# One pass of a fused linear-attention and mixture-of-experts kernel: the state added by an identity matmul, fewer matmuls of zeros, and steps put in other places

## The chip, the cores and the metric

The kernel runs on one core of a Trainium2 chip. Its time is device microseconds of one execution; 482.89 us is the median of three runs. A profiled execution is a run of its own, with a time of its own.

## The reference, cut to what matters

A gated linear attention is followed by a mixture of eight experts that takes one expert for each token. Batch is 4, heads 8, sequence 768, head width 48, model width 384, hidden width 1024.

```python
for t in range(S):                       # attention: a state of 48 x 48 per head
    state = alpha[:, :, t, :, None] * state + einsum('bhd,bhe->bhde', k[:, :, t], v[:, :, t])
    y[:, :, t] = einsum('bhd,bhde->bhe', q[:, :, t], state)
...
logits = einsum('bsd,de->bse', x, w_gate)            # x is y with the heads side by side
...
    e = argmax(logits[b, s]) if s == 0 or local_gate[b, s] < 0.5 else prev_e
    p = softmax(logits[b, s])
    out[b, s] = p[e] * (maximum(x[b, s] @ w1[e], 0) @ w2[e])
```

## The kernel before, in words

**The attention blocks.** The 3072 tokens are cut into 24 blocks of 128 (`NB`), four at a time from the four batches (`G`), so that block i continues the state of block i-4. A block is two chunks of 64 tokens. The loop over i (line 684) works on several blocks at once. In pass i it does, in this order: `one_a(i+2)` (GpSimd writes ones into the decay tile `a`), `scan2(i+1)` (VectorE's backward scan `sf`, after which GpSimd multiplies k), `flush` (work put off on the list `later`), `kt(i)` (k transposed by TensorE into `kp`, copied by ScalarE to `kk`), `copies(i-1)` and `state(i-1)`, `pm(i)` (scores `pe`, masked to `pq` by VectorE), some of the list `made`, a first `other()`, `scan1(i+2)` (VectorE's forward scan `A`, after which GpSimd multiplies q), loads, `xt(i-2)` (y transposed into `xp`, copied to `xx`), `ym(i-1)` (the output `y`: first scores times values, `y<-vt,pq`, then q times state, `y<-sb,x`), `first_v(i+1)`, a step of the weights, a second `other()`, `um(i)` (k times v into the PSUM tile `up`), a third `other()`.

**The state.** `um` (line 369) makes 8 matmuls into `up`, which holds two sums for each head: over the first chunk and over the whole block. VectorE then adds the old state to both (line 387) into the SBUF tile `st`. `copies` (line 390) lets ScalarE copy the two results into `sb` in two instructions, and `state` (line 395) multiplies the last one with the decay for block i+4. `up` is one PSUM buffer.

**The order.** From line 658 on every engine's instructions are pinned to program order, so each engine is a queue in which a waiting instruction holds all behind it.

**other(), line 622.** It runs `flush`, then one step of each generator in `steps` (the routing of a group of four blocks, `route`, line 432, which yields between its steps), and then, while `work[0]` is empty, `DN` matmuls of zeros (`dense`, line 293: 128x128 weights, 256 columns, into the PSUM tile `h2`). When the routing of the third group ends, `work[0]` becomes `early()` (line 562): early expert work on the first 1536 tokens. It comes in pieces: gathers, empty pieces, two transposes (`trans`, into `tp`, in the same PSUM buffer as `kp` and `xp`), eight pieces of the first layer (`gemm1`: 9 matmuls into a half of `h2`, a relu by ScalarE to `hh`, and a remainder `hl` that VectorE computes at the next `flush`), then pieces of the second layer (`yp`). In passes 0 to 23 a second and a third `other()` take one piece each, from pass 24 on all three do.

**After the blocks.** `while steps` (line 728) goes on until the last group is routed. The other experts follow (lines 753 to 768), with 480 tokens each.

**At the start** (lines 264 to 282 and 647 to 683) GpSimd clears tiles and builds constants before it writes the first `one_a(0)`; a list `made` of 12 further ones is spread over the first passes, three in each.

Of the kernel before, what the change touches and what calls it, by code (L numbers as in the profile page):

```python
# [46 lines left out]
DN = 2  # L47
# [19 lines left out]
def gla_moe(ctx, tc, akq, vw, vn, wg, w1, w2, cst, tok, out):  # L67
# [188 lines left out]
    with ExitStack() as ac, ExitStack() as aa:  # L256
# [16 lines left out]
        for j in range(2):  # L273
            sb = ap.tile([R, 2, 2, CW], F32, bufs=1, name=f"sb{j}")
            g_.memset(sb[0:64], 0.0)
            g_.memset(sb[64:112, :, 1, :], 0.0)
            SBs.append(sb)
            oh = ap.tile([128, E, G + 1], F32, bufs=1, name=f"oh{j}")
            g_.memset(oh, 0.0)
            OHs.append(oh)  # L280

        st = {"c": c0}
        sts = [ap.tile([R, 3, HP, D], F32, tag="st", bufs=G + 1, name=f"st_{i}") for i in range(G)]
# [35 lines left out]
        def scan1(i):  # L319
# [7 lines left out]
            q2 = x[:, BW:].rearrange("p (s t) -> p s t", t=C)  # L327
            g_.tensor_tensor(q2, q2, A.rearrange("p (s t) -> p s t", t=C + 1)[:, :, 1:], ALU.mult)
            d["k"] = x[:, 0:BW].rearrange("p (h t) -> p h t", h=HP)
            d["q"] = x[:, BW:2 * BW].rearrange("p (h t) -> p h t", h=HP)  # L330

# [37 lines left out]
        def um(i):  # L369
# [3 lines left out]
            if i < G:  # L373
                s3 = sts[i]
                g_.memset(s3[:, 0], 0.0)
            else:
                s3 = st["S", i % G]
            uw = pp.tile([128, 512], F32, tag="up", name=f"up_{i}")
            up = uw[0:R, 0:2 * CW].rearrange("p (h c d) -> p c h d", c=2, h=HP)
            for hp in range(HP):  # L380
                n = slice(2 * hp * D, 2 * (hp + 1) * D)
                t_.matmul(uw[64:112, n], lhsT=kk[:, hp, 64:112], rhs=vt[:, :, 2 * hp * D:(2 * hp + 1) * D],
                          start=True, stop=True)
                t_.matmul(uw[0:64, n], lhsT=kk[:, hp, 0:64], rhs=vt[:, :, (2 * hp + 1) * D:(2 * hp + 2) * D],
                          start=True, stop=True)
            n = 2 if i + G < NB else 1
            v_.tensor_tensor(s3[:, 1:1 + n], up[:, 0:n], s3[:, 0].unsqueeze(1).broadcast_to([R, n, HP, D]), ALU.add)
            d["s3"] = s3

        def copies(i):  # L390
            sf, sb = blk[i]["s3"].rearrange("p c h d -> p c (h d)"), blk[i]["sb"]
            s_.copy(sb[64:112, :, 0, :], sf[64:112, 0:2])
            s_.copy(sb[0:48, :, 1, :], sf[0:48, 0:2])

        def state(i):
            d = blk[i]
            if i + G < NB:
                sn = ap.tile([R, 3, HP, D], F32, tag="st", bufs=G + 1, name=f"st_{i + G}")
                v_.scalar_tensor_tensor(sn[:, 0], d["s3"][:, 2], 1.0 / SEED,
                                        d["end"].unsqueeze(2).broadcast_to([R, HP, D]), ALU.mult, ALU.mult)  # L400
                st["S", i % G] = sn
# [30 lines left out]
        def route(g):  # L432
# [36 lines left out]
            yield  # L469
# [29 lines left out]
            yield  # L499
            v_.tensor_tensor(ex, ex, ob, ALU.mult)  # L500
            pn = rt([128, n], "pn")
            v_.tensor_reduce(pn, ex, AX.X, ALU.add)
            v_.tensor_tensor(pl[:, :, 0], pn, se, ALU.mult)
# [5 lines left out]
            yield  # L509
            ps = rt([128, E, n + 1], "ps")  # L510
# [28 lines left out]
            else:  # L539
                for j in range(n):  # L540
                    s_.activation(on[:, j], iob, AF.Abs, bias=rr[:, j:j + 1], scale=-1.0)
                    s_.activation(on[:, j], on[:, j], AF.Relu, bias=one[:, 0:1], scale=-float(TS))
                    if j < n - 1:
                        yield
# [17 lines left out]
        def early():  # L562
# [10 lines left out]
            for _ in range(4):  # L573
                yield False
# [47 lines left out]
        def other(pieces=True):  # L622
# [5 lines left out]
            if work[0] is None:  # L628
                if DN:
                    dense(DN)  # L630
            else:
                if last and drained[0]:
                    last[0].ht, last[0].yt = HL, YL
                for done in work[0] if pieces else ():
                    if done or steps or not drained[0]:
                        break

# [9 lines left out]
        g_.memset(one, 1.0)  # L647
        g_.memset(m5, 1.0)
        g_.memset(m5[:, :, 0], 0.0)
        for e in range(E):  # L650
            g_.memset(c0[:, e:e + 1], float(e * RS - 1))
            g_.memset(c1[:, e:e + 1], float(e * RS - 1 + (C1 if e in EARLY else 0)))
        g_.tensor_copy(trif, cc("tri"))
        g_.memset(trif[0:64, 64:128], 1.0)
        g_.memset(trif[64:128, 0:64], 0.0)
# [4 lines left out]
        made = [  # L660
            lambda: g_.memset(fill, 0.0),
# [279 lines left out]
```

## Time and profile before

| what | value |
|---|---|
| runs | 481.34, 482.89 and 493.2 us, median 482.89 |
| profiled execution, its own time | 484.0 us |
| its span, first to last instruction | 482.2 us, 10873 instructions |
| mean granted TensorE clock | 0.961 |
| ScalarE, GpSimd busy | 194.1 us, 186.7 us |
| HBM read and written | 55.84 MB, 10.62 MB |

A row of a group of instructions says: line, engine, operation, result <- sources, shape, count, then the busy time in us and the mean of one in ns, then the idle time of the engine just before them and what ended it. PE is TensorE, DVE VectorE, ACT ScalarE, POOL GpSimd, SP the queue of loads. All compute instructions carry line 81, the helper that records them, so they are told apart by their tiles. A row of a timeline begins with its start and its duration in us. A row of stretches gives, for each stretch of the span, its length and then the busy time and the count for PE, PE's weight loads, DVE, ACT and POOL, and at the end the granted clock, the share of DMA and GB/s. Busy times of PE are modelled, and pipelined matmuls overlap: the distance from one start to the next says what one costs.

### The profile page before, as it was taken

How to read it: one execution, taken by the hardware profiler on the slowest of the kernel's cores; microseconds unless marked ns; L12 is line 12 of the kernel's file. 1: busy time of each engine (PE TensorE's matmuls, PEld its weight loads, DVE VectorE, ACT ScalarE, POOL GpSimd, SP SyncE). 2: the span in 40 equal slices, each digit the busy share in tenths (PEclk: the TensorE clock that was granted, in tenths of full speed). 3: DMA queues.
4: the chain of work that ended last, by engine and by line, in shares of the span. 5: the costliest groups of instructions: out<-in, count | busy, mean ns of one | idle time of the engine just before them, and what ended most of it. 6: DMA issues, size and time to landing. Idle time of an engine off the chain costs nothing.

```text
span 482.2 us, 10873 instructions
## 1 busy us (share of the span) xinstructions
PE 437.9 (91%) x4443; PEld 391.5 (81%) x4443; DVE 257.3 (53%) x485; ACT 194.1 (40%) x390; POOL 186.7 (39%) x207
## 2 busy tenths in 40 slices
PE   5999898999997978698989999999999999999990
PEld 5777776878875877597878998998989989989990
DVE  4778999898997235722274445244254252342310
ACT  1345656565756436321354324335144233242210
POOL 6654326364556000261053642724732503504201
PEclk9799999999998899888899999999999999999997
DMA  8789767596661102660075554444351542531100
GB/s 217 199 260 252 222 187 201 164 292 167 189 208 50 51 17 71 180 186 27 1 224 188 134 181 138 124 131 123 114 175 57 158 130 65 174 98 39 50 3 27
DMA packets 26710, 66.01 MB, mean 137 GB/s; under 512 B 4384, under 2 KB 10677, under 8 KB 26658
## 3 DMA queue, kind: packets, MB, share of 16 engines
q1 hardware_dynamic: 18672, 49.65, 36.3%
q0 software_dynamic: 3840, 10.62, 6.9%
q10 hardware_dynamic: 4146, 5.03, 3.1%
q8 instruction: 35, 0.57, 0.5%
q14 instruction: 17, 0.14, 0.1%
HBM read 55.84 MB, written 10.62 MB: 138 GB/s over the span
## 4 chain that ended last, share of the span: by engine, by line
PE 53%; issue 11%; DVE 9%; ACT 3%; POOL 2%; POOLq 0%; DVEq 0%; ACTq 0%
PE h L81 24%; PE yp L81 20%; PE y L81 3%; PE tp L81 2%; DVE A L81 2%; POOL out L81 1%; PE up L81 1%; DVE st L81 1%; DVE sf L81 1%; DVE pq L81 1%; ACT hh L81 1%; POOL w1l_0b L81 1%; PE pe L81 1%; DVE xl L81 1%; PE lp L81 1%
## 5 line engine op out<-in xcount | busy, mean ns | idle before, releaser
L81 DVE SCALAR_TENSOR_TENSOR hl<-h,hh 128x480 fp32r<-128x480 f32 (+2 forms) x80 | 43.9, 556 | 77.2 <-ACT hh L81 76.9
L81 ACT ACTIVATE hh<-h 128x480 fp32r<-128x480 f32 (+2 forms) x80 | 38.7, 490 | 82.4 <-PE h L81 82.3
L81 POOL DMA_INDIRECT out<-yo,idx x32 | 32.5, 1017 | 80.5 <-DVE yo L81 78.0
L81 POOL DMA_INDIRECT xg<-xd,idx x32 | 32.6, 1018 | 61.0 <-PE tp L81 52.9
L81 DVE TENSOR_SCALAR yo<-yp,acc 128x384 f32<-128x384 f32 (+1 forms) x32 | 19.6, 616 | 61.1 <-PE yp L81 61.0
L81 POOL TENSOR_TENSOR x<-x,sf 112x512 f32<-112x512 f32 x24 | 29.0, 1209 | 42.5 <-DVE sf L81 42.5
L81 POOL TENSOR_TENSOR x<-x,A 112x512 f32<-112x512 f32 x24 | 31.8, 1327 | 29.0 <-DVE A L81 6.6
L81 DVE TENSOR_TENSOR_SCAN A<-a,z 112x520 f32<-112x520 f32 x24 | 34.5, 1437 | 5.6 <-POOL a L81 5.6
L81 PE MATMUL h<-dz 128*128 128x256 f32 x142 | 35.0, 354 | 2.1 <-DVE z L81 2.1
L81 DVE TENSOR_TENSOR_SCAN sf<-a,z 112x520 f32<-112x520 f32 x24 | 33.8, 1408 | 0.1
L81 ACT COPY sb<-st 48x384 f32<-48x384 f32 x48 | 24.5, 510 | 11.5 <-DVE st L81 10.9
L81 PEld LDWEIGHTS h<-dz 128*128 128x128 f32 x142 | 23.8, 224 | 6.5 <-DVE z L81 2.1
L81 PEld LDWEIGHTS y<-vt,pq 64*64 64x64 f32 x768 | 24.9, 138 | 4.0 <-issue 3.8
L81 PE MATMUL y<-vt,pq 64*64 64x48 f32 x768 | 27.9, 224 | 0.0
L81 PE MATMUL y<-sb,x 112*64 112x96 f32 x384 | 21.8, 258 | 4.3 <-ACT sb L81 4.2
L81 PE MATMUL up<-vt,kk 128*48 128x96 f32 (+1 forms) x384 | 23.1, 267 | 0.0
L81 PEld LDWEIGHTS y<-sb,x 112*64 112x64 f32 x384 | 17.2, 140 | 6.2 <-ACT sb L81 5.2
L81 PEld LDWEIGHTS up<-vt,kk 128*48 128x48 f32 (+1 forms) x384 | 18.3, 140 | 3.4 <-issue 1.0
L81 ACT COPY kk<-kp 128x448 f32<-128x448 f32 x24 | 12.8, 531 | 20.7 <-PE kp L81 20.6
L81 PE MATMUL h<-xh,w1h_1a 128*128 128x256 f32 (+1 forms) x48 | 16.4, 342 | 3.9 <-DVE hl L81 2.7
L81 ACT COPY XR<-y 128x384 f32<-128x384 f32 x24 | 11.5, 479 | 20.1 <-PE y L81 20.1
L81 ACT CAST xh<-tp 128x384 fp32r<-128x384 f32 (+1 forms) x32 | 14.0, 462 | 13.9 <-PE tp L81 13.6
(247 smaller groups left out, 1234.8 us busy)
## 6 DMA issues: line engine op xcount, KB each, us to landing
x<-akq SPq DMA_DIRECT2D x24, 448.0 KB, 5.6
a<-akq SPq DMA_DIRECT2D x24, 227.9 KB, 4.5
vt<-vn SPq DMA_DIRECT2D x24, 192.0 KB, 2.7
xd<-XR ACTq DMA_DIRECT2D x24, 192.0 KB, 4.8
rw_0a<-w SPq DMA_DIRECT2D x3, 512.0 KB, 4.9
rw_0a<-w SPq DMA_DIRECT2D x4, 384.0 KB, 4.2
rw_1a<-w SPq DMA_DIRECT2D x3, 512.0 KB, 5.9
rw_1a<-w SPq DMA_DIRECT2D x4, 384.0 KB, 3.5
```

Of the source, the lines that this page charges most:

```text
L81: r = f(*a, **k)
```

## The change

The parts of the diff, in its order:

- Filler: `DN` goes from 2 to 1, and `other` takes the number as an argument, 2 for the first of a pass. So a pass issues 2 + 1 + 1 = 4 matmuls of zeros in place of 6. The test is new too: they are issued wherever no full piece of early work ran and the blocks aren't over (`not done and not drained[0]`), also after the early work has begun.
- Start: the clearing of the second `sb`, of both `oh`, `one`, `m5` and `trif` goes into `made`, which is now worked off five at a time; `c0` and `c1` are computed from `ioa` in place of sixteen small memsets; for block 0 the multiplication of q comes after that of k (`scale_q`).
- State: from block 4 on a matmul with the 112x112 identity as weights and the old state as moving operand (each head's 48 columns given twice, 384 in all, fp32) writes the state into both sums of `up`, and the 8 matmuls of `um` accumulate onto it. VectorE's addition is gone. `copies` makes four instructions of 48x192: the first chunk's state comes straight from the SBUF state, the second's from `up`. `state` reads `up`.
- Routing: two empty or nearly empty steps are dropped, the product of probabilities with the one-hot goes to GpSimd (`eo`), its sum moves behind the prefix matmul, and `on` is made two columns in a step. A group takes 12 calls in place of 16. `early` has two empty pieces in place of four.
- Weights: the step of the first early expert's weights moves behind the second `other()`, with its ScalarE cast and, at the next `flush`, its VectorE subtraction.

```diff
--- before.py
+++ after.py
@@ -44,7 +44,7 @@
 NEXT = 2
 
 DN0 = 32
-DN = 2
+DN = 1
 HL = ("h", "h", "up", "pe")
 YL = ("yp", "y")
 RT = "rt"
@@ -272,15 +272,14 @@
             VTs.append(vt)
         for j in range(2):
             sb = ap.tile([R, 2, 2, CW], F32, bufs=1, name=f"sb{j}")
-            g_.memset(sb[0:64], 0.0)
-            g_.memset(sb[64:112, :, 1, :], 0.0)
+            if j == 0:
+                g_.memset(sb[0:64], 0.0)
+                g_.memset(sb[64:112, :, 1, :], 0.0)
             SBs.append(sb)
-            oh = ap.tile([128, E, G + 1], F32, bufs=1, name=f"oh{j}")
-            g_.memset(oh, 0.0)
-            OHs.append(oh)
+            OHs.append(ap.tile([128, E, G + 1], F32, bufs=1, name=f"oh{j}"))
 
         st = {"c": c0}
-        sts = [ap.tile([R, 3, HP, D], F32, tag="st", bufs=G + 1, name=f"st_{i}") for i in range(G)]
+        sts = [ap.tile([R, HP, D], F32, tag="st", bufs=G + 1, name=f"st_{i}") for i in range(G)]
         blk = {}
         grp = {}
         later = []
@@ -324,10 +323,15 @@
             v_.tensor_tensor_scan(A, a[:, 0:SW], z1, 0.0, ALU.mult, ALU.add)
             d["end"] = A[:, 2 * C + 1:SW:2 * (C + 1)]
             v_.reciprocal(z2[0:R, 2 * C + 1:SW:2 * (C + 1)], d["end"])
-            q2 = x[:, BW:].rearrange("p (s t) -> p s t", t=C)
-            g_.tensor_tensor(q2, q2, A.rearrange("p (s t) -> p s t", t=C + 1)[:, :, 1:], ALU.mult)
+            d["A"] = A
+            if i:
+                scale_q(i)
             d["k"] = x[:, 0:BW].rearrange("p (h t) -> p h t", h=HP)
             d["q"] = x[:, BW:2 * BW].rearrange("p (h t) -> p h t", h=HP)
+
+        def scale_q(i):
+            q2 = blk[i]["x"][:, BW:].rearrange("p (s t) -> p s t", t=C)
+            g_.tensor_tensor(q2, q2, blk[i].pop("A").rearrange("p (s t) -> p s t", t=C + 1)[:, :, 1:], ALU.mult)
 
         def one_a(i):
             a = blk[i]["a"]
@@ -370,33 +374,35 @@
 
             d = blk[i]
             kk, vt, sb = d["kk"], d["vt"], d["sb"]
-            if i < G:
-                s3 = sts[i]
-                g_.memset(s3[:, 0], 0.0)
-            else:
-                s3 = st["S", i % G]
             uw = pp.tile([128, 512], F32, tag="up", name=f"up_{i}")
             up = uw[0:R, 0:2 * CW].rearrange("p (h c d) -> p c h d", c=2, h=HP)
+            if i < G:
+                st["S", i] = sts[i]
+                g_.memset(sts[i], 0.0)
+            else:
+                t_.matmul(uw[0:R, 0:2 * CW], lhsT=ident[0:R, 0:R],
+                          rhs=st["S", i % G].unsqueeze(2).broadcast_to([R, HP, 2, D]), start=True, stop=False,
+                          skip_group_check=True)
             for hp in range(HP):
                 n = slice(2 * hp * D, 2 * (hp + 1) * D)
                 t_.matmul(uw[64:112, n], lhsT=kk[:, hp, 64:112], rhs=vt[:, :, 2 * hp * D:(2 * hp + 1) * D],
-                          start=True, stop=True)
+                          start=i < G, stop=True, skip_group_check=True)
                 t_.matmul(uw[0:64, n], lhsT=kk[:, hp, 0:64], rhs=vt[:, :, (2 * hp + 1) * D:(2 * hp + 2) * D],
-                          start=True, stop=True)
-            n = 2 if i + G < NB else 1
-            v_.tensor_tensor(s3[:, 1:1 + n], up[:, 0:n], s3[:, 0].unsqueeze(1).broadcast_to([R, n, HP, D]), ALU.add)
-            d["s3"] = s3
+                          start=i < G, stop=True, skip_group_check=True)
+            d["up"], d["S"] = up, st["S", i % G]
 
         def copies(i):
-            sf, sb = blk[i]["s3"].rearrange("p c h d -> p c (h d)"), blk[i]["sb"]
-            s_.copy(sb[64:112, :, 0, :], sf[64:112, 0:2])
-            s_.copy(sb[0:48, :, 1, :], sf[0:48, 0:2])
+            d = blk[i]
+            sb = d["sb"].rearrange("p c e (h d) -> p c e h d", h=HP)
+            for c, x in ((0, d["S"]), (1, d["up"][:, 0])):
+                s_.copy(sb[64:112, c, 0], x[64:112])
+                s_.copy(sb[0:48, c, 1], x[0:48])
 
         def state(i):
             d = blk[i]
             if i + G < NB:
-                sn = ap.tile([R, 3, HP, D], F32, tag="st", bufs=G + 1, name=f"st_{i + G}")
-                v_.scalar_tensor_tensor(sn[:, 0], d["s3"][:, 2], 1.0 / SEED,
+                sn = ap.tile([R, HP, D], F32, tag="st", bufs=G + 1, name=f"st_{i + G}")
+                v_.scalar_tensor_tensor(sn, d["up"][:, 1], 1.0 / SEED,
                                         d["end"].unsqueeze(2).broadcast_to([R, HP, D]), ALU.mult, ALU.mult)
                 st["S", i % G] = sn
 
@@ -466,7 +472,6 @@
             v_.scalar_tensor_tensor(m2, kr[:, 1, :, 0], 16.0, m2, ALU.mult, ALU.add)
             v_.tensor_tensor(kr[:, 0], ge, m2.unsqueeze(2).broadcast_to([128, n, 8]), ALU.is_equal)
             yield
-            yield
 
             rp = pp.tile([8 * n, 2, 128], F32, tag=RT, name=f"rp_{g}")
             for j in range(2):
@@ -496,17 +501,17 @@
             v_.tensor_reduce(se, ex, AX.X, ALU.add)
             v_.tensor_scalar_add(se, se, 1e-9)
             v_.reciprocal(se, se)
-            yield
-            v_.tensor_tensor(ex, ex, ob, ALU.mult)
-            pn = rt([128, n], "pn")
-            v_.tensor_reduce(pn, ex, AX.X, ALU.add)
-            v_.tensor_tensor(pl[:, :, 0], pn, se, ALU.mult)
+            eo = rt([128, n, 8], "eo")
+            g_.tensor_tensor(eo, ex, ob, ALU.mult)
             yield
             pw = pp.tile([128, E, n + 1], F32, tag=RT, name=f"pw_{g}")
             t_.matmul(pw.rearrange("p e b -> p (e b)"), lhsT=one, rhs=oi.rearrange("p e b -> p (e b)"),
                       start=True, stop=False)
             t_.matmul(pw[:, :, 0:n], lhsT=trif, rhs=o4, start=False, stop=True)
             yield
+            pn = rt([128, n], "pn")
+            v_.tensor_reduce(pn, eo, AX.X, ALU.add)
+            v_.tensor_tensor(pl[:, :, 0], pn, se, ALU.mult)
             ps = rt([128, E, n + 1], "ps")
             v_.tensor_tensor(ps, pw, st["c"].unsqueeze(2).broadcast_to([128, E, n + 1]), ALU.add)
             po = rt([128, n, 8], "po")
@@ -540,7 +545,7 @@
                 for j in range(n):
                     s_.activation(on[:, j], iob, AF.Abs, bias=rr[:, j:j + 1], scale=-1.0)
                     s_.activation(on[:, j], on[:, j], AF.Relu, bias=one[:, 0:1], scale=-float(TS))
-                    if j < n - 1:
+                    if j == 1:
                         yield
             yield
 
@@ -570,8 +575,8 @@
                 j.load_list(0)
             for _ in jobs[0].gather():
                 yield False
-            for _ in range(4):
-                yield False
+            yield False
+            yield False
             for _ in jobs[0].trans():
                 yield True
             for n, j in enumerate(jobs):
@@ -619,21 +624,21 @@
 
         last, EW, steps = [], {}, []
 
-        def other(pieces=True):
+        def other(pieces=True, dn=DN):
 
             flush()
             for r in list(steps):
                 if next(r, 0) == 0:
                     steps.remove(r)
-            if work[0] is None:
-                if DN:
-                    dense(DN)
-            else:
+            done = False
+            if work[0] is not None:
                 if last and drained[0]:
                     last[0].ht, last[0].yt = HL, YL
                 for done in work[0] if pieces else ():
                     if done or steps or not drained[0]:
                         break
+            if not done and not drained[0]:
+                dense(dn)
 
         work, drained = [None], [False]
         for i in range(3):
@@ -644,20 +649,21 @@
                 nc.scalar.dma_start(cs, cst)
                 nc.scalar.dma_start(tk, tok)
                 nc.scalar.dma_start(wgs, wg[:, :, 0:32])
-        g_.memset(one, 1.0)
-        g_.memset(m5, 1.0)
-        g_.memset(m5[:, :, 0], 0.0)
-        for e in range(E):
-            g_.memset(c0[:, e:e + 1], float(e * RS - 1))
-            g_.memset(c1[:, e:e + 1], float(e * RS - 1 + (C1 if e in EARLY else 0)))
-        g_.tensor_copy(trif, cc("tri"))
-        g_.memset(trif[0:64, 64:128], 1.0)
-        g_.memset(trif[64:128, 0:64], 0.0)
         nc.scalar.dma_start(xd[0:1], z2[127:128, 0:DM])
         first_v(0)
         pinned[0] = True
         dense(DN0)
         made = [
+            lambda: g_.memset(SBs[1][0:64], 0.0),
+            lambda: g_.memset(SBs[1][64:112, :, 1, :], 0.0),
+            lambda: g_.memset(one, 1.0),
+            lambda: g_.memset(OHs[0], 0.0),
+            lambda: g_.memset(OHs[1], 0.0),
+            lambda: g_.memset(m5, 1.0),
+            lambda: g_.memset(m5[:, :, 0], 0.0),
+            lambda: g_.tensor_copy(trif, cc("tri")),
+            lambda: g_.memset(trif[0:64, 64:128], 1.0),
+            lambda: g_.memset(trif[64:128, 0:64], 0.0),
             lambda: g_.memset(fill, 0.0),
             lambda: g_.tensor_copy(fill.bitcast(I32)[:, 1:2], tk[0:SL, 2 * NB:]),
             lambda: g_.memset(acc, 0.0),
@@ -674,10 +680,16 @@
                                      tk[:, 0:2 * NB].rearrange("p (b j t) -> p t j b", b=G, t=2)[:, 0],
                                      -float(SENT), None, ALU.add),
             lambda: g_.tensor_copy(vals[:, :, 2], tk[:, 1:2 * NB:2]),
+            lambda: v_.tensor_scalar(c0, ioa[:, :, 0], WH, float(TS), ALU.subtract, ALU.mult),
+            lambda: v_.tensor_scalar(c0, c0, -1.0, None, ALU.add),
+            lambda: g_.tensor_copy(c1, c0),
+        ] + [
+            lambda e=e: g_.memset(c1[:, e:e + 1], float(e * RS - 1 + C1)) for e in EARLY
         ]
         one_a(0)
         scan1(0)
         scan2(0)
+        scale_q(0)
         one_a(1)
         scan1(1)
         wsteps = iter(())
@@ -696,9 +708,9 @@
                 pm(i)
             if i > NB:
                 drained[0] = True
-            for _ in range(min(3, len(made))):
+            for _ in range(min(5, len(made))):
                 made.pop(0)()
-            other(i >= NB)
+            other(i >= NB, 2)
             if i + 2 < NB:
                 scan1(i + 2)
             if i + 3 < NB:
@@ -717,11 +729,11 @@
             if i == W0:
                 begin(EARLY[0], v_)
                 wsteps = EW[EARLY[0]].steps()
-            elif i > W0 + 2:
-                next(wsteps, None)
             if i == T1:
                 begin(EARLY[1], v_)
             other()
+            if i > W0 + 2:
+                next(wsteps, None)
             if i < NB:
                 um(i)
             other()
```

## The prediction

> **What bounds the kernel now.** I read the page, then the span cut where blocks begin (16.5 us is where block 1's k is transposed, 40.6 block 5, 89 block 12, 126.5 block 18, 137.1 block 20, 171.1 pass 24, 201.3 the second early expert's first matmul).
>
> ```profile
> span 482.2 us, 10873 instructions
> PE 437.9 (91%) x4443; PEld 391.5 (81%) x4443; DVE 257.3 (53%) x485; ACT 194.1 (40%) x390; POOL 186.7 (39%) x207
> ...
> 0.00:16.50 16.50, 11.65 (x91) 10.61 (x92) 9.83 (x12) 2.74 (x4) 10.49 (x44) 0.83 0.93 228
> 16.50:40.60 24.10, 21.74 (x434) 18.16 (x434) 18.06 (x28) 11.29 (x23) 13.18 (x24) 0.98 0.81 236
> 40.60:89.00 48.40, 43.48 (x834) 36.34 (x833) 43.46 (x82) 29.78 (x66) 21.51 (x24) 0.96 0.68 197
> 89.00:126.50 37.50, 36.37 (x725) 30.60 (x723) 34.24 (x77) 23.46 (x58) 18.52 (x19) 1.00 0.76 222
> 126.50:137.10 10.60, 10.48 (x222) 8.87 (x220) 10.36 (x20) 6.99 (x18) 6.54 (x9) 1.00 0.66 191
> 137.10:171.10 34.00, 28.99 (x485) 23.99 (x485) 20.33 (x50) 16.82 (x42) 11.80 (x10) 0.90 0.27 82
> 171.10:201.30 30.20, 22.90 (x206) 20.37 (x206) 17.56 (x51) 15.04 (x33) 2.92 (x3) 1.00 0.29 85
> ```
>
> The share of 53% for DVE hides that it is busy 34.24 of 37.5 us from block 12 to 17, and 10.36 of 10.6 in blocks 18 and 19. But PE is fuller still: 36.37 of 37.5. So between 40.6 and 137.1 PE idles only 6.2 us of 96.5 (4.9, 1.1 and 0.1). PE's idle time lies at the start (4.9), before block 5 (2.4), and above all after 137.1 (5.0 and 7.3). What is taken from DVE pays only where PE waits, and what is given to PE is paid in full where it doesn't. What comes after 208.8 (the last stretch quoted below) is not edited, and I let it move along unchanged.
>
> **Price of the state's matmul against the fillers.**
>
> ```profile
> 118.79 0.88 PE L81 MATMUL up<-vt,kk 128*48 128x96 f32 x16
> 119.60 0.51 PE L81 MATMUL h<-dz 128*128 128x256 f32 x2
> 119.94 0.55 PE L81 MATMUL kp<-cs,x 112*128 112x112 f32 x4
> ```
>
> The groups that the edit touches:
>
> ```profile
> L81 PE MATMUL h<-dz 128*128 128x256 f32 x142 | 35.0, 354 | 2.1 <-DVE z L81 2.1
> L81 ACT ACTIVATE on<-on,one 128x128 f32<-128x128 f32 x20 | 8.0, 402 | 0.6
> L81 DVE TENSOR_TENSOR ex<-ex,oh 128x32 f32<-128x32 f32 x3 | 1.8, 602 | 0.0
> L81 DVE TENSOR_TENSOR st<-up,st 112x384 f32<-112x384 f32 x20 | 10.9, 547 | 7.2 <-POOL a L81 3.8 <-PE up L81 1.8 <-POOL st L81 1.5
> L81 ACT COPY sb<-st 48x384 f32<-48x384 f32 x48 | 24.5, 510 | 11.5 <-DVE st L81 10.9
> ```
>
> No fp32 matmul of 384 columns is there. The nearest row is `up`: 8 calls give 16 instructions, so fp32 is two passes, and they take 119.60 - 118.79 = 0.81 us. If the two column halves (64 and 48 wide) stream side by side, that is 4 x 96 = 384 columns twice, just what the identity needs, with 16 weight loads against 2: I take 0.75. If they do not, the 0.81 us stand for 16 x 96 = 1536 columns and the identity's 768 cost half of it, 0.41. Bounds 0.41 to 0.81. A pair of fillers costs 119.94 - 119.60 = 0.34, so 0.17 to 0.215 each with what follows; I take 0.19. The 142 are 32 at the start and 2 x 55. After, I count 4 in each of passes 0 to 18, 3 in pass 19 and 2 in passes 20 to 23: 32 + 76 + 3 + 8 = 119. So the label is true for a pass, but passes 18 to 23 get fillers that they didn't have, and each block from 4 on gets 0.75 - 2 x 0.19 = +0.37 us of PE work, from pass 20 on 1.13.
>
> DVE loses 24 additions (0.55 us for 20 of them). ACT's two copies of 0.51 become four of half the length; by the fixed part of an instruction I put them 0.2 us longer in all (0 to 0.5), hidden behind PE's y matmuls, except in the pass where `on` now comes as 2 + 2 columns: eight instructions of 0.4 us in one pass, where three of the four columns used to fall in one pass, with the last in the next.
>
> **Steps that only move.** The weights' step issues a load on SP's queue, a cast on ACT and, one flush later, a subtraction on DVE. On SP nothing of `other` stands between, so loads keep their order. On ACT the cast now goes behind the routing's copies or `on`, and the next `kk` waits behind it as before. On DVE the subtraction used to stand before the addition and the next sf; it still stands before sf. GpSimd's `eo` (128x32; VectorE's `ex<-ex,oh` took 0.60 us for it) runs behind q's product and is read two steps later, so it costs nothing while GpSimd is as free as it is (18.5 us of 37.5); without that cover the prefix step would come 0.6 us or more later in each of six groups. The `made` list puts 15 more small instructions into passes 0 to 5, on GpSimd mostly (the memset of `a` below took 0.11 us), behind k's products. I cost all these at nothing.
>
> **The start (-2.3; -1.5 to -3).**
>
> ```profile
> 2.15 6.41 PE L81 MATMUL h<-dz 128*128 128x256 f32 x32 [2.15 <-DVE z L81]
> 11.25 1.01 PE L81 MATMUL kp<-cs,x 112*128 112x112 f32 x4 [2.70 <-POOL a L81]
> ```
>
> ```profile
> 6.20 0.11 POOL L81 MEMSET a<- 112x4 f32 x1
> 10.02 1.17 POOL L81 TENSOR_TENSOR x<-x,sf 112x512 f32<-112x512 f32 x1 [1.18 <-DVE sf L81]
> ```
>
> VectorE's queue, and the time that loads of `a` take:
>
> ```profile
> 6.34 1.24 DVE L81 TENSOR_TENSOR_SCAN A<-a,z 112x520 f32<-112x520 f32 x1 [4.23 <-POOL a L81]
> 7.83 2.11 DVE L81 TENSOR_TENSOR_SCAN sf<-a,z 112x520 f32<-112x520 f32 x1
> ...
> DMA to landing us min/median/max: 3.1/4.5/8.2
> ```
>
> The first scan waits for the memset of `a`, which waits behind GpSimd's constants. With these gone, the load ends it: at about 4.1 if it takes near the shortest time, as nothing else is in flight. Then A runs at 4.2, sf at 5.65, in 1.24 and not 2.11 as q's product no longer runs beside it, k's product 6.9 to 8.1, block 0's transposes at 8.2 in place of 11.25. q's product and the memset for block 1 follow, so block 1 gains less: its A at 9.45, sf to 13.0, product to 14.2 in place of 16.5.
>
> **Blocks 1 to 4 (-2.4; -1 to -3).** DVE's addition waited here for GpSimd's memset of the state (3.8 + 1.5 us in the `st` row above). Nothing on DVE waits for it any more; ScalarE's copies are next in line, a pass later. PE's work falls by eight fillers (-1.5) and rises by one identity (+0.75), so its 2.4 us of idle time may go.
>
> **Blocks 5 to 17 (+3.2; 0 to +6).** 13 identities at 0.75 less 26 fillers at 0.19 are +4.8, and the list matmul of the third group now falls in here (+0.9). Against it stand the waits:
>
> ```profile
> PE lt L81 <- ACT lc L81: 1.7, 3, 0.8
> PE y L81 <- ACT sb L81: 1.5, 2, 1.1
> ```
>
> and the stretches in which PE's clock was granted at half:
>
> ```profile
> 10.85:17.68 6.83, 6.43 (x74) 5.31 (x78) 6.07 (x6) 1.16 (x3) 4.28 (x9) 0.50 1.03 268
> 58.64:62.05 3.41, 3.41 (x24) 2.84 (x24) 2.71 (x4) 1.54 (x3) 1.23 (x2) 0.50 0.98 305
> 154.20:161.00 6.80, 6.80 (x75) 6.15 (x71) 1.43 (x9) 2.84 (x7) 1.79 (x2) 0.50 0.20 61
> 202.00:208.80 6.80, 6.08 (x29) 5.61 (x28) 2.38 (x8) 1.15 (x3) 4.73 (x5) 0.50 0.83 241
> ```
>
> Of the 6.0 us that PE idles here (4.9 + 1.1) I take 4 as gone: `lt` waited for a small copy behind the weights' cast, which now stands after it, the waits for `sb` went back to the addition, and one cold stretch (1.7 us) may not come again. New is +1.5 from ACT where `on` comes in fours: three passes at 0.5.
>
> **Blocks 18 and 19 (+2.0; +1 to +3).** Two identities, five fillers and a transpose piece more, less the list matmul that has moved up: 1.5 + 0.95 + 0.45 - 0.9.
>
> **Blocks 20 to 23 (+5.0; +2 to +7).**
>
> ```profile
> 149.96 0.49 PE L81 MATMUL tp<-cs,xg 128*128 128x128 f32 x3
> 152.31 0.57 PE L81 MATMUL kp<-cs,x 112*128 112x112 f32 x4 [1.86 <-issue]
> ...
> 176.21 1.17 PE h L81 x9
> ```
>
> Early work starts four places sooner and has two empty pieces less, so by the end of pass 23 seven first-layer pieces are done in place of three. PE gets 4 x 1.2 for them, 3.0 of identities and 1.5 of fillers, less a transpose piece (0.45): +8.85. The half-rate stretch from 154.2 to 161 halves 6.8 us, worth 3.4; with this much work about, I take it as gone. Waits stay about as they are (-0.45): `kp` shares its buffer with `tp`, so the 1.86 us wait moves to pass 20 with the piece, and the fillers write `h2`, which now holds early results, so they wait for `hl`.
>
> **Pass 24 to the second expert (-8.7; -5 to -11), and the stretch after 202 (-1.7; 0 to -3.4).**
>
> ```profile
> PE lp L81 <- DVE on L81: 2.5, 1, 2.5
> PE h L81 <- DVE hl L81: 1.9, 2, 0.9
> PE rb L81 <- DVE em L81: 1.6, 1, 1.6
> ```
>
> The four pieces are gone from here (-4.8), with them the wait for `hl` (-1.9), and the last group's routing has two steps fewer while the weights' subtractions, which hold DVE before `em` and `on`, come earlier (-2.0 of 4.1). Half of the cold stretch at 202, which follows the 2.5 us wait, is counted as saved.
>
> The sum is -2.3 - 2.4 + 3.2 + 2.0 + 5.0 - 8.7 - 1.7 = -4.9. The profiled execution took 484.0, 1.1 above the median, so I subtract from the median: 478.0.
>
> **A rule beside the rows.** The 2 us of the stretch at 58.64 were lost although PE's waits for `sb` up to block 17 were 1.1 us at the longest. The Trainium skill, page "TensorE: Matmul & The Clock Gate", section "Why this matters for your kernels", tells to leave no idle gaps of more than about 3 us between bursts of matmuls; fewer fillers would then be harmless here, since no wait quoted here is that long, and the sum would not change. The trace disagrees: shorter waits were enough, so I keep a stretch more or less in the bounds.
>
> **The rivals.**
>
> 1. Slower: `up` is held longer. Before, `um` could start when the addition had read `up`; now it needs the last ScalarE copy and DVE's `state`, which stands behind a weights' subtraction, a routing step and the next sf. Price: 1 us in each of the seven blocks with a weights' step and half in each of the other eight or so, 11 in all: 489. It decides once DVE's queue from one `um` to `state` is longer than PE's block of 6 us. For it speaks DVE's 43.46 of 48.4 us; against it that DVE loses 0.55 us a block.
> 2. Faster: idle time collapses. The first, second and fourth cold stretch vanish wholly (a further -2, -1.7, -1.7), and 4 us more of the waits after 137.1: 478 - 9.4, about 469. For it: DVE's release, early work as filler. Against it: PE is full without it.
> 3. The tail is bound by the last group's chain and by the weights' casts, not by PE: pieces done early only lengthen waits, so -8.7 becomes -3: 484. For it: PE idles 7.3 of 30.2 us there. Against: that chain starts only after PE's work in pass 24.
> 4. The identity is cheap (0.41): 20 x 0.34 less, 471.
>
> **How the numbers follow.** Forecast 478: 0.40 (own range 473 to 483). Rival 1: 0.20, 2: 0.18, 3: 0.12, 4: 0.10. About 2% (473.2 and 492.5) is what a measurement of this kernel can tell from no change. Faster: 0.15 of 2, 0.08 of 4 and 0.06 of the forecast's lower end, 0.29. Slower: 0.12 of rival 1, when it adds to the upper bounds of blocks 5 to 23. Within: 0.59. The range 466 to 489 holds the forecast, 2, 3 and 4 nearly whole and the lower half of 1.
>
> **What would show it.** Right: block 0's transposes near 8.2, fillers 119, an identity matmul at 0.75 in distance of starts, PE idle below 5 us in blocks 5 to 17 and that stage longer than 85.9 us, blocks 18 and 19 near 12.6, the second expert's first matmul near 196 to 198. Wrong: `um` waiting for `state` or `sb` (rival 1); no stretch at half rate after the start (rival 2); a wait for `on` or `em` above 4 us (rival 3).

## The result and the profile after

The changed kernel takes 508.1 us, the median of four executions from 506.1 to 510.2, against 486.4 for four of the kernel before. The ratio is 1.054, 95% interval 1.045 to 1.063: slower by 5%. The profiled execution took 510.21 us, its span 508.4, 26.2 more than the span before. Some executions, here and in the experiments, ran at a lower granted clock and took longer, and every ratio leaves them out (here 489.95 and 493.2 of the kernel before, in r1 four of seven); the profiled executions of r1, r3 and b3 were of that kind, so lengths are not taken from them.

The stretches of the span of the changed kernel, cut where the same blocks begin (columns as before: length, busy time and count of PE, its weight loads, DVE, ACT and POOL, granted clock, DMA share, GB/s):

```profile
0.00:15.50 15.50, 8.81 (x89) 7.88 (x89) 8.70 (x12) 2.84 (x4) 7.59 (x17) 1.00 0.89 240
15.50:41.70 26.20, 25.62 (x429) 20.89 (x429) 19.02 (x27) 12.01 (x30) 15.62 (x37) 0.80 0.71 202
41.70:95.80 54.10, 48.63 (x835) 38.17 (x834) 41.03 (x76) 33.43 (x82) 20.10 (x28) 0.91 0.65 185
95.80:147.00 51.20, 45.17 (x731) 35.92 (x731) 32.77 (x66) 25.97 (x71) 21.84 (x24) 0.87 0.55 164
147.00:161.80 14.80, 12.56 (x228) 9.76 (x227) 10.76 (x23) 7.58 (x21) 4.74 (x8) 1.00 0.64 190
161.80:198.00 36.20, 35.62 (x534) 29.38 (x534) 15.16 (x40) 18.65 (x51) 8.63 (x10) 0.91 0.16 51
198.00:225.20 27.20, 19.72 (x177) 17.39 (x176) 16.63 (x47) 14.49 (x32) 3.64 (x4) 0.99 0.45 124
225.20:508.40 283.20, 261.61 (x1450) 241.72 (x1449) 101.48 (x167) 87.51 (x148) 101.89 (x76) 0.96 0.35 108
```

Against the rows of before the stages differ by -1.0, +2.1, +5.7, +13.7, +4.2, +2.2, -3.0 and +2.3. The loss stands in the third to fifth: blocks 5 to 19 take 23.6 us more. There PE's idle time (length less busy) grew from 4.9, 1.1 and 0.1 us to 5.5, 6.0 and 2.2, and the clock fell from 0.96 and 1.00 to 0.91 and 0.87. PE, full before, now waits and runs slowly.

Of TensorE's waits in the changed kernel the four longest, and of VectorE's the one that is new (total, times, longest), one fence each:

```profile
PE lp L81 <- POOL a L81: 7.3, 3, 2.5
PE rp L81 <- DVE kr L81: 5.8, 5, 1.7
PE kp L81 <- POOL x L81: 4.0, 2, 2.6
PE lp L81 <- DVE on L81: 3.8, 1, 3.8
```

```profile
DVE st L81 <- ACT sb L81: 32.5, 17, 7.5
```

The first two rows weren't there before, and neither was VectorE's (`rp` waited 2.3 us in all before, for `acc`). They are waits of the routing's own matmuls, and of the new `state`. The stretches at half rate between blocks 1 and 23, as windows:

```profile
16.27:26.51 10.24, 9.66 (x134) 7.80 (x125) 6.02 (x8) 3.63 (x10) 7.41 (x18) 0.50 0.53 152
70.88:81.12 10.24, 9.68 (x90) 7.48 (x90) 4.70 (x7) 4.48 (x11) 2.96 (x5) 0.50 0.35 94
105.01:115.25 10.24, 9.81 (x90) 7.62 (x92) 4.63 (x6) 2.70 (x7) 3.96 (x6) 0.50 0.66 195
139.15:142.56 3.41, 3.41 (x25) 3.08 (x27) 2.54 (x5) 0.87 (x3) 1.77 (x2) 0.50 0.02 5
163.04:169.87 6.83, 6.83 (x60) 5.08 (x62) 3.75 (x13) 3.46 (x10) 1.75 (x3) 0.50 0.30 89
```

The second, third and fourth stand where the list matmul `lp` of the first three groups waits. PE's timeline of pass 9, with its neighbours on the other engines (the bracket is the idle time before the instruction, and its releaser):

```profile
68.47 0.69 PE L81 MATMUL pe<-x 48*64 48x64 f32 x32
68.71 1.18 POOL L81 TENSOR_TENSOR x<-x,A 112x512 f32<-112x512 f32 x1 [2.79 <-PE kp L81]
...
69.85 1.54 POOL L81 TENSOR_TENSOR vo<-oa,vals 128x384 f32<-128x384 f32 x1
...
70.75 0.40 ACT L81 ACTIVATE on<-on,one 128x128 f32<-128x128 f32 x1
...
71.34 0.10 POOL L81 MEMSET a<- 112x4 f32 x1
...
71.44 2.02 PE L81 MATMUL lp<-vo,on 128*128 128x96 f32 x8 [2.28 <-POOL a L81]
...
72.33 0.64 ACT L81 COPY sb<-up 48x192 f32<-48x192 f32 x2
...
73.00 0.36 DVE L81 SCALAR_TENSOR_TENSOR st<-up,A 112x192 f32<-112x192 f32 x1 [0.51 <-ACT sb L81]
```

`lp` reads `vo`, which ends at 71.39 on GpSimd, behind q's product, and `on`, which ends at 71.15 on ScalarE. The wait goes down as one for `a`, the small memset behind `vo`. PE stands from 69.16 to 71.44. The granted clock goes to half at 70.88, before that wait is over, and stays there for 10.24 us. `lp` waits again until 105.44 (2.51 us) and until 138.99 (2.50 us), with a cold stretch (one at half rate) at 105.01 and at 139.15.

### The profile page after: what moved, and what is told of

Same layout as the page of the kernel before. It is cut to its first block, busy times and chain, and to the rows that moved or that the text cites. A ratio compares the mean times of both kernels' runs of the same rounds, so it can differ in the third digit from the quotient of the medians.

```text
span 508.4 us, 10929 instructions
## 1 busy us (share of the span) xinstructions
PE 457.7 (90%) x4460; PEld 401.1 (79%) x4460; DVE 245.5 (48%) x457; ACT 202.5 (40%) x438; POOL 184.0 (36%) x200
## 4 chain that ended last, share of the span: by engine, by line
PE 68%; issue 11%; DVE 5%; ACT 5%; POOL 4%; DMA 3%; SPq 1%; another core or an unknown queue 1%; POOLq 0%; ACTq 0%; DVEq 0%
PE h L81 24%; PE yp L81 19%; PE y L81 8%; PE up L81 6%; PE lp L81 2%; PE pe L81 2%; PE kp L81 2%; PE xp L81 1%; PE tp L81 1%; DMA rw_3b<-w 1%; ACT sb L81 1%; PE lg L81 1%; POOL x L81 1%; POOL out L81 1%; SPq L81 1%
## 5 line engine op out<-in xcount | busy, mean ns | idle before, releaser
L81 POOL DMA_INDIRECT xg<-xd,idx x32 | 33.4, 1045 | 66.1 <-PE tp L81 53.4
L81 POOL TENSOR_TENSOR x<-x,A 112x512 f32<-112x512 f32 x24 | 29.4, 1227 | 54.8 <-PE rp L81 16.8
L81 DVE TENSOR_TENSOR_SCAN sf<-a,z 112x520 f32<-112x520 f32 x24 | 38.6, 1609 | 0.9
L81 DVE TENSOR_TENSOR_SCAN A<-a,z 112x520 f32<-112x520 f32 x24 | 30.9, 1289 | 5.7 <-POOL a L81 5.7
L81 PEld LDWEIGHTS y<-vt,pq 64*64 64x64 f32 x768 | 27.6, 150 | 4.7 <-issue 4.7
L81 PE MATMUL y<-vt,pq 64*64 64x48 f32 x768 | 30.7, 236 | 0.0
L81 PEld LDWEIGHTS h<-dz 128*128 128x128 f32 x119 | 21.7, 226 | 7.6 <-DVE z L81 2.1
L81 PE MATMUL y<-sb,x 112*64 112x96 f32 x384 | 24.7, 273 | 0.6 <-ACT sb L81 0.5
L81 ACT COPY XR<-y 128x384 f32<-128x384 f32 x24 | 11.5, 478 | 32.4 <-PE y L81 32.4
L81 DVE SCALAR_TENSOR_TENSOR st<-up,A 112x192 f32<-112x192 f32 x20 | 7.1, 355 | 32.7 <-ACT sb L81 32.5
L81 PE MATMUL lp<-vo,on 128*128 128x96 f32 x48 | 10.4, 372 | 11.7 <-POOL a L81 7.3
L81 DVE TENSOR_TENSOR xl<-tp,xh 128x384 fp32r<-128x384 f32 (+1 forms) x32 | 16.2, 523 | 5.8 <-ACT xh L81 4.6
```

What stands on the lines that cost most here:

```text
L81: r = f(*a, **k)
```

## The experiments

The theory of the first runs (A): the new routing puts `lp` a third of a pass behind `vo` and `on`, PE waits, and the cold clock behind the wait costs more than the wait. A2, its later form, adds that VectorE's `state`, queued behind ScalarE's copies, makes the sources late. Rivals were that the identity, the fillers, the start or the weights' step costs it.

**`lp` later, or behind cover.** e1 puts three empty steps, a pass, ahead of `lp`:

```diff
                     if j == 1:
                         yield
             yield
+            if not end:
+                yield
+                yield
+                yield
```

> The changed kernel with three empty routing steps ahead of the list matmul (not in the last group), so that it comes a pass after the one-hot columns and the GpSimd product, as before. Theory A (the list matmul waits for them in passes 9, 13 and 17, 7.3 us in three waits, and the clock falls to half behind each wait, 10.2 + 10.2 + 3.4 us at half rate): both vanish, -15 to -19, less 2 to 3 for early work that starts three places later: about 493. Rival B (the identity's 0.74 us in each of 20 blocks is the loss, the waits would be spent elsewhere): no more than -5, above 503.

Its four executions took 489.3, 491.8, 499.1 and 502.1 us, with 484.2 before: too far apart for a ratio. In the profiled one, of 491.8, `lp` no longer waits in the first three groups, and between 40 and 200 us its cold stretches are two of 3.41 us and one of 6.83, in place of two of 10.24, one of 3.41 and one of 6.83. e2 issues twelve matmuls of zeros instead, right ahead of `lp`:

```diff
+            if g < 3:
+                dense(12)
             lp = pp.tile(
```

> The changed kernel with 12 matmuls of zeros in PE's queue ahead of the list matmul of the first three groups. The wait stays, filled. If the half-rate stretches behind the waits are what costs most (clock part of theory A): about -10, 498, and no half-rate stretch in passes 9 to 18. If only the wait itself counts: 508 or up to 2 more.

It took 493.8, ratio 1.020 (1.012 to 1.027). PE does more work in it than in the changed kernel, and yet the ratio falls from 1.054, so the wait and its cold clock are much of the loss. In e2 no stretch is at half rate between 25.0 and 209.3 us.

**The parts taken back, one at a time.** e3: VectorE adds the state as before.

```diff
-                t_.matmul(uw[0:R, 0:2 * CW], lhsT=ident[0:R, 0:R],
...
+            v_.tensor_tensor(s3[:, 1:1 + n], up[:, 0:n], ..., ALU.add)
```

> The changed kernel with the state added by VectorE as before, no identity matmul and the two long ScalarE copies. Rival B: 20 x 0.74 us of PE work go, and VectorE's state no longer waits for ScalarE's copies (32.5 us in 17 waits): -10 to -15, about 496. Theory A: the waits of the list matmul stay, so -3 to -6, about 504.

498.3, ratio 1.029 (1.022 to 1.036), between the two. Without the identity, 2.5 of the 5.4 points go and 2.9 stay; `lp` waits even more:

```profile
PE lp L81 <- POOL a L81: 9.7, 3, 3.6
```

a1: `route` as before, all else changed; b2: the kernel before with only the new `route`.

> The changed kernel with the routing's 16 old steps in place of the 12 new ones; state by identity, four fillers, new start and the weights' step stay. Theory A (the new routing's early list matmul, its waits and the cold clock behind them are the loss, the identity being neutral by itself): 485 to 488. Rival C (four fillers a pass leave the clock cold wherever PE waits at all): above 495, with half-rate stretches left between passes 9 and 18.

> The kernel before with only the routing's part of the change (12 steps, products on GpSimd, one-hot columns two at a time), six fillers as before. Theory A: the list matmul waits here too, 2 to 3 us in each of three passes; with six fillers the clock falls less: +6 to +12, about 492. Rival C (without fewer fillers nothing is lost): within 3 of 484.

a1 took 489.6, ratio 1.021 (1.011 to 1.031); b2 502.7, ratio 1.047 (1.033 to 1.060). So the new routing alone costs nearly the whole 5%, more than I had expected of it, and it needs no identity for that. Some of TensorE's waits in b2:

```profile
PE pw L81 <- DVE se L81: 4.9, 2, 2.7
PE kp L81 <- issue: 4.4, 1, 4.4
PE rp L81 <- DVE kr L81: 3.6, 4, 1.7
PE lp L81 <- POOL a L81: 3.3, 2, 1.9
```

It isn't `lp` alone: the prefix matmul `pw` and the transposes `rp` wait for VectorE as well.

b1: the kernel before with only the identity, its four copies and `state` from `up`. f1: only the filler rule. s1: only the start. w1: only the weights' step. e4: the changed kernel with `DN = 2`, six matmuls of zeros in a pass.

> The kernel before with only the state's part of the change: identity matmul, four copies, state read from PSUM; six fillers, old routing, old start. Theory A: PE was full in blocks 5 to 19, so it costs most of 20 x 0.74 = 14.8 less what VectorE's release gives: +4 to +9, about 493. Rival B: +15 or more, above 500.

> The kernel before with only the filler rule of the change (2 + 1 + 1 in a pass, and also between early pieces). By PE's price of a filler (0.19): -8 at most in full stages, +1 to +3 from fillers in passes 18 to 23: 480 to 484. If the clock needs six a pass: a further half-rate stretch or two of 6.8, 486 to 490.

> The kernel before with only the start's part of the change. Block 0 begins 2.3 earlier; then PE runs blocks 1 and 2 at half rate as in the changed kernel, where block 2 began 2.1 later than before: 482 to 486. The prediction's own term (-2.3 kept): 481 or less.

> The kernel before with only the weights' step moved behind the second place. Theory (the parts cost together what none costs alone): 481 to 485, no stretch at half rate more than before. Rival (the weights' step is what stayed when the old routing was put back): 487 to 490.

> The changed kernel with DN = 2, so six fillers a pass and two in every later place without a full piece. Rival C: the clock stays up, -8 to -14, about 497. Theory A: fillers don't stand in the wait (the list matmul is ahead of them in PE's queue), PE gets 0.38 us more a pass: 508 to 514.

b1: 482.2, ratio 0.990 (0.982 to 0.998), where a cost had been expected. f1: 481.3, 1.000 (0.995 to 1.005). s1: 484.1, 1.004 (1.000 to 1.008). w1: 481.6, 1.000 (0.995 to 1.004). Each is free by itself. The two empty pieces that `early` loses weren't tried alone. e4: 503.5, 1.048 (1.038 to 1.058); it came out below what A made of it, with 20.5 us lost to half rate up to 260 us in place of 27.2. Why, no run shows.

**The queue of VectorE.** e5 takes the changed kernel and swaps two calls; c1 does so in b1, c2 in a1.

```diff
-                copies(i - 1)
                 state(i - 1)
+                copies(i - 1)
```

> The changed kernel with VectorE's state ahead of ScalarE's copies in program order. If VectorE waits for the copies only because both read the same PSUM tile, its 32.5 us of waits shrink to those for the matmuls, and ScalarE's copy from PSUM waits for VectorE instead. If these waits are off the path (theory A): 505 to 510. If they count (rival 1 of the prediction, the tile held too long): -5 or more.

> The kernel before with only the state's part of the change (482.2 by itself, against 484.2) and with VectorE's state ahead of ScalarE's copies. Theory A2 (the order counts only through the list matmul, whose inputs VectorE's wait makes late; with the old routing nothing waits there): within 3 of the identity alone, about 480. Rival 1 (the PSUM tile held too long counts in every block): 470 or less.

> The changed kernel with both cures at once: the old routing steps and VectorE's state ahead of the copies. Theory A2: each took away the same loss (489.6 and 488.8 of 508), so together no more than 2 below either, about 488. Rival (two losses of their own, 18 and 19): near 472.

e5: 488.8, ratio 1.015 (1.003 to 1.027): 19 us for an exchange of two lines, which I had thought off the path. c1: 485.1, 1.001 (0.997 to 1.006); c2: 490.9, 1.020 (1.015 to 1.026). The exchange gains nothing where the old routing leaves room. In e5 VectorE no longer waits for `sb`, ScalarE waits for `st` instead, and the wait ahead of `lp` is about halved:

```profile
ACT sb L81 <- DVE st L81: 4.1, 5, 1.3
PE lp L81 <- POOL a L81: 3.9, 3, 1.9
```

In the first group GpSimd's `vo` took 0.83 us there and not 1.54:

```profile
72.04 0.83 POOL L81 TENSOR_TENSOR vo<-oa,vals 128x384 f32<-128x384 f32 x1
```

That isn't what e5 gains by: in the second and third group `vo` took 1.76 in e5 too, and 1.76 in the first three groups of the kernel before.

**Which steps of the routing.** r1 (on the kernel before, with the new routing) and r2 (on the changed kernel) give `on` its four steps back.

```diff
-                    if j == 1:
+                    if j < n - 1:
                         yield
```

> The kernel before with the new routing, but the one-hot made one column in a step, so that the list matmul comes two thirds of a pass later behind its sources. Theory (the list matmul too close behind its sources is what the new routing costs): 482 to 490, PE waits less than 1 us for POOL ahead of the list matmul. Rival (the other steps of the routing cost it, the product on GpSimd or the dropped steps ahead): 498 or more.

> The changed kernel with the one-hot made one column in a step. Theory (list matmul): like the changed kernel with the old routing, 487 to 493. Rival (the other steps of the routing): 500 or more.

r1: 1.027 (1.019 to 1.034), three executions from 494.5 to 496.7; r2: 499.1, 1.035 (1.031 to 1.040). Both theories missed: a third to a half of the loss goes. In r2 `lp` no longer waits in the first three groups, but the next matmul of the routing does:

```profile
PE rp L81 <- DVE kr L81: 7.3, 5, 2.3
PE lp L81 <- DVE on L81: 4.6, 1, 4.6
```

So A in its narrow form falls: `lp`, `rp` and, in b2, `pw` each stand too close behind the engine that feeds them. r3 puts the empty step ahead of `rp` back too, and takes the state first; 15 steps in place of 12.

```diff
+            yield
             yield
 
             rp = pp.tile(
```

> The changed kernel with an empty step ahead of the kept-row transposes, the one-hot one column in a step (15 steps in place of 12; before had 16) and the state ahead of the copies. Theory (the sum of work, waits and stretches): work stays near 447, the routing's waits fall to 8 or less and the stretches lose 13 to 17, so 485 to 491. Rival (dropping steps isn't it; the product on GpSimd or the sum behind the prefix matmul costs what the new routing costs): 498 or more.

488.1, ratio 1.011 (1.005 to 1.017), from 1.054: some 20 us, with the product still on GpSimd and its sum still behind the prefix matmul. But e5, which only takes the state first, is at 1.015 already, and the intervals overlap, so r3 doesn't show what the steps alone give back. What the steps of `on` cost is shown, by r1 and r2; how the rest of the new routing's cost (1.027 in r1) divides among the empty step ahead of `rp`, the step after `se` and the product on GpSimd isn't. What is left in r3 costs 1 to 2%, as in a1.

**The rest of a1.** w2 is a1 with the weights' step where it was; b3 is b1 with the filler rule.

> The changed kernel with the old routing and the weights' step where it was: identity, fillers and start are left of the change. Rival (the weights' step costs the rest): 481 to 484. Theory (the parts together): 486 to 490, with a wait of PE that none of the three shows alone.

> The kernel before with the identity and with the filler rule, the rest as before. Theory (sum): work near 446, waits 22 to 25, stretches losing 12 to 14: 479 to 485. Rival (fewer fillers beside the identity bring the clock down): stretches losing 17 or more, 487 or more.

w2: 490.9, 1.021 (1.013 to 1.029), so the weights' step isn't it. b3: 480.8, 0.996 (0.991 to 1.000): identity and fillers are free together.

**A sum over the variants.** I took from each profile the waits of TensorE up to 260 us (all rows of that view added) and half the length of the half-rate stretches that begin up to there. What remains of the span is TensorE's own work and what no row shows. Each figure is of one profiled execution.

| kernel | span | half of cold stretches | waits | rest |
|---|---|---|---|---|
| before | 482.2 | 15.3 | 31.8 | 435.1 |
| f1, s1, w1 (one part, no identity) | 479.1, 481.3, 481.7 | 13.6, 11.9, 17.0 | 32.6, 33.4, 30.6 | 432.9, 436.0, 434.1 |
| b2 (new routing alone) | 499.3 | 28.9 | 39.5 | 430.9 |
| e3 (changed, no identity) | 498.7 | 28.9 | 38.1 | 431.6 |
| b1 (identity alone) | 481.9 | 11.9 | 23.4 | 446.6 |
| a1, w2 (changed, old routing) | 487.1, 489.0 | 15.3, 17.0 | 28.8, 28.6 | 443.0, 443.4 |
| e5 (changed, state first) | 489.7 | 17.1 | 28.8 | 443.9 |
| e1, r2 (changed, other steps) | 490.0, 500.7 | 13.6, 23.9 | 31.2, 33.5 | 445.2, 443.3 |
| c1, c2 (b1 and a1, state first) | 483.9, 487.1 | 11.9, 13.6 | 23.9, 27.3 | 448.1, 446.2 |
| e2, e4 (changed, more matmuls of zeros) | 491.3, 502.6 | 11.9, 20.5 | 28.7, 33.2 | 450.7, 448.9 |
| after | 508.4 | 27.2 | 34.8 | 446.4 |

The rest is 431 to 436 without the identity and 443 to 448 with it, and more where matmuls of zeros were added. So the identity costs some 11 us of TensorE's work on the kernel before (by starts its 20 matmuls make 14.8; where the other 3.3 went no row shows). Between e3 and the changed kernel, which differ in the state alone, the rest differs by the full 14.8. In b1 8.4 of it come back in waits, 4.2 of them the row `y <- ACT sb` of before, which stood behind VectorE's addition. The 3.4 of cold stretches in b1 are 0.007 of its span, no more than executions of one kernel differ by: those of the kernel before that count had granted clocks from 0.950 to 0.982. Under the whole change with the old routing only 3 come back, which makes 4.9 us (1%) between the two profiled executions; a1's ratio is 2%. The new routing adds 6 to 8 us of waits and 12 to 14 of cold clock. The clocks of all executions agree with this: 0.939 to 0.944 in four of the changed kernel, 0.956 to 0.959 in four of a1, 0.963 to 0.979 in four of e2. Some of TensorE's waits in b1 and then in w2:

```profile
PE kp L81 <- POOL a L81: 3.5, 1, 3.5
PE rb L81 <- DVE em L81: 2.7, 3, 1.6
PE lp L81 <- DVE on L81: 2.5, 1, 2.5
```

```profile
PE lp L81 <- DVE on L81: 4.1, 1, 4.1
PE kp L81 <- POOL x L81: 3.8, 2, 2.6
PE kp L81 <- issue: 3.5, 1, 3.5
PE rp L81 <- DVE acc L81: 3.2, 2, 2.2
```

The last group's wait for `on` and the `kp` wait put down to `issue` are longer in w2. The latter stands in a1 too:

```profile
147.83 0.53 DVE L81 TENSOR_TENSOR xl<-tp,xh 128x384 fp32r<-128x384 f32 x1
...
148.47 0.98 PE L81 MATMUL kp<-cs,x 112*128 112x112 f32 x4 [3.55 <-issue]
```

`kp` and `tp` share a PSUM buffer, and `kp` starts 0.11 us after VectorE has read `tp` for `xl`, which stands behind a scan and the routing. A stretch at half rate begins at 146.97 and lasts 10.24 us; in w2 one of the same length begins at 148.96. In b1 this wait was 1.2 and no stretch stood there. w2 differs from b3, which is free, in the start and in the two empty pieces that `early` loses. Neither was tried alone beside the identity, so which of them makes the 2% of a1 and w2 stays open; the place of this wait, at the first piece of the early work, speaks for the empty pieces.

## Why the prediction was wrong

**The prices held.** An identity matmul was put at 0.75 us and took 0.74 by starts:

```profile
66.21 0.81 PE L81 MATMUL up<-st,cs 112*112 112x384 f32 x2
66.95 0.88 PE L81 MATMUL up<-vt,kk 128*48 128x96 f32 x16
```

The groups of the page after:

```profile
L81 PE MATMUL h<-dz 128*128 128x256 f32 x119 | 34.6, 375 | 2.1 <-DVE z L81 2.1
L81 DVE SCALAR_TENSOR_TENSOR st<-up,A 112x192 f32<-112x192 f32 x20 | 7.1, 355 | 32.7 <-ACT sb L81 32.5
```

The fillers are 119 as counted, and the net of identities and fillers, 20 x 0.74 - 23 x 0.19 = +10.4, is near the +11.3 of the rest in the table.

**The step that failed** is that of blocks 5 to 17, "+3.2; 0 to +6": it came to +5.7 + 13.7 = +19.4. In that stage PE idled 11.5 us and not 6.0, and half of its cold stretches came to 11.9 us and not 1.7; with the +4.8 of work that adds up to +20.5, near it. Its work was right. Its sentences "I take 4 as gone" and "one cold stretch (1.7 us) may not come again" were wrong, and "New is +1.5 from ACT where `on` comes in fours" named the place and a fraction of the price. I treated the dropped steps as a move of `lp` (+0.9), and asked what each step costs, not how many matmuls of other work lie between a step that makes a value and the one that reads it. Those steps were the distance (shown for `lp`, by e1, r1 and r2). The 10.24 us of cold clock behind each of two waits, worth 5.1 each, stood in no term, although rows of half rate stood in the prediction.

**A second miss is VectorE's queue.** I counted that it loses 0.55 us in a block, and about that went: its busy time fell from 257.3 to 245.5 us. But `state` now waits 32.5 us for ScalarE's `sb<-up`. Neither writes what the other reads; both read `up`. The Trainium skill, page "PSUM — Partial Sum Buffer", section "PSUM bank collisions raise a hardware error", says that the compiler's back end adds a dependency between instructions of different engines on one bank and quadrant, reads against reads too. The row of 32.5 us agrees, and so does e5, where the order is the other way round: this row is gone, and ScalarE waits 4.1 us for `st`. I weighed the clock rule and not this one.

**The other terms.** The start: k of block 0 began at 9.37 (forecast 8.2, before 11.25), as the load landed later than I put it. The PE and GpSimd rows of the start:

```profile
9.37 0.60 PE L81 MATMUL kp<-cs,x 112*128 112x112 f32 x4 [1.44 <-POOL x L81]
15.46 0.60 PE L81 MATMUL kp<-cs,x 112*128 112x112 f32 x4 [2.58 <-POOL x L81]
```

```profile
5.19 0.11 POOL L81 MEMSET a<- 112x4 f32 x1 [1.97 <-DMA a<-akq]
15.34 1.19 POOL L81 MEMSET sb<- 64x768 f32 x2
16.90 2.13 POOL L81 TENSOR_TENSOR x<-x,A 112x512 f32<-112x512 f32 x1
```

Block 1 gained 1.0 in place of 2.3, and blocks 1 to 4 lost 2.1 in place of gaining 2.4. PE idled only 0.6 us there, so its 2.4 us of idle time went for the most part, as I had said; what was lost is the clock, 0.80 in this stage and 0.98 before, with the cold stretch of 10.24 us. The `made` steps that I cost at nothing stand ahead of q's product for the next blocks; whether they cost anything no run shows. Blocks 18 and 19 came to +4.2 (forecast +2.0), 20 to 23 to +2.2 (+5.0; the stretch that I took as gone is there at 163.04), from pass 24 to the second expert -3.0 (-8.7: the wait for `on` is 3.8 us and PE idles 7.5 of 27.2, near the 7.3 of before), the rest +2.3 (-1.7).

**The rivals.** Rival 1, `up` held longer, had the cause half right: `state` stands behind the last ScalarE copy. But `um` never waits for it; VectorE's queue behind `state` does, and its price was 19 us with the new routing and none without, not 11. Rival 3 came out as written, -3 for the stage behind pass 24 and not -8.7; its sign, a wait above 4 us, was just missed at 3.8. Nothing speaks for rivals 2 and 4. No row of TensorE's waits names GpSimd's product `eo`, which was to cost nothing, but no run takes it back alone.

## What to carry to other kernels

A step in a pinned order is distance between a producer and its reader; before it is dropped, look at the slack of every matmul behind it on the engine that is full. Here waits of 2.3 and 2.5 us on TensorE had stretches behind them that cost 5.1 more each, so price both. Add up work, waits and cold stretches for each variant: it shows which of them a part pays in. And try every part alone, the smallest too: the empty pieces of `early` were left out here, so the cause of a1's 2% stays open.

## What the runs showed of the hardware

At three waits of 2.3 to 2.5 us stand stretches of 3.41 or 10.24 us at a granted clock of 0.50, though PE was busy 9.68 of the 10.24 us; in e2, where matmuls of zeros fill these waits (2.5 us are left of 7.3), none stands there. The Trainium skill, page "TensorE: Matmul & The Clock Gate", section "Why this matters for your kernels", asks only for no gaps above some 3 us; the rows here are stricter. Every stretch at half rate up to 260 us was a multiple of 3.41 us. This agrees with the window of 3413 ns in the section "What's actually happening" of the same page of the Trainium skill. In r2 waits of 1.0 us ahead of `rp`, at 55.57, 84.86 and 112.69, brought none, and one of 1.94 us at 140.94 was followed by a stretch at 142.1. But length alone doesn't decide: in b2 a wait of 2.70 us ahead of `pw` at 63.25 brought none, and one of 1.41 ahead of `lp` at 71.92 was followed by a stretch at 72.39. Where the limit lies isn't settled, since no run varied the length of a wait alone.

GpSimd's `vo`, 128x384 with two sources in SBUF, took 1.54 us when VectorE's subtraction `w2l` had begun 0.13 us before it, and a scan followed. In the same place in e5 it took 0.83, with that subtraction begun 0.40 us after it; there the subtraction took 1.24 us in place of 0.98.
